# A fused recurrence, gated layer and soft mixture of experts: outputs in column parts for all token tiles, and another order of the same steps

## The chip, the cores and the metric

The kernel runs on one core of a Trainium2 chip, from loading the inputs in HBM to the last output byte in HBM, as one program. The metric is the device time of one execution in microseconds (us); smaller is better. The kernel before took 550.89 us, the median of three runs that lie between 550.50 and 551.18 us.

## The reference: what is computed

The inputs r, k, v, w have the shape [4, 8, 768, 48] (batch, heads, positions, features of a head), u has [8, 48], all float32. The weights w_in [384, 2048] and w_out [2048, 384] arrive as float64; phi [384, 32], w1 [8, 384, 1024] and w2 [8, 1024, 384] are float32. There are three parts.

```python
for t in range(S):                                   # 1. recurrence over 768 positions
    cur = einsum('bhd,bhe->bhde', u * k[t], v[t])
    y[t] = einsum('bhd,bhde->bhe', r[t], state + cur)
    state = w[t][..., None] * state + einsum('bhd,bhe->bhde', k[t], v[t])
x = y.transpose(0, 2, 1, 3).reshape(3072, 384)       # 3072 tokens
h = x @ w_in                                         # 2. gated layer
x = (h * cos(h)) @ w_out
logits = x @ phi                                     # 3. soft mixture of experts, 32 slots
d = softmax of logits over the 3072 tokens           #    (a column each)
slot_input = d.T @ x                                 #    [32, 384], 4 slots for each of 8 experts
slot_out[e] = relu(slot_input[e] @ w1[e]) @ w2[e]
c = softmax of logits over the 32 slots              #    (a row each)
out = c @ slot_out                                   #    [3072, 384] float32, 4.72 MB
```

Because d is a softmax over all tokens, no row of the output can be computed before the last token has gone through parts 1 and 2.

## The kernel before

**One list sets the order.** Most of the program is a string HEAD of 1977 names such as `h.11.5.0`, each a small function with its arguments. A loop runs through them inside `manual_schedule`, and every instruction then stands on its engine in the order in which the list issued it: an engine that waits for one of its instructions lets all later ones wait. The DMA triggers on SyncE (SP) go by the same list. After the list comes the tail, written out in Python, where order is set in the same way.

**Recurrence.** The tokens are cut into 24 blocks of 128 (two chunks of 64 in each head). For block j the steps are: loads (`lw`, `lk`, `lr`, `lv`, `lz`), transposes on TensorE (`wT`, `kT`, `rT`, `kN`), scans of the decays on VectorE (`scan`, L156, and `sp`), scaled keys and receptances (`ks`, `L`), the product of the two inside a chunk (`A`, TensorE) and its triangular mask (`mask`, L222, VectorE), the bonus sum (`ru` on GpSimd, `bo`, L243, on VectorE, `bv`), the update of the state (`U`, L259, TensorE, 0.88 us, then `z`, `st`, `rz`), the output (`y`, `yb`), and its two halves in a rounded format (`xh`, `xl`).

**Weights.** The float64 weights are turned into float32 on the chip by integer operations on their bits. For each of eight blocks n of w_in (`.i.n`) and of w_out (`.o.n`) the list has a load `raw`, a pass `abs` on ScalarE (L353), then `mx` (L357), `d1`, `d2a` and `d2b` (L374) on VectorE. Blocks of w_out are afterwards transposed on TensorE (`oT.m`, L416, three 128x128 tiles each, two of them per block), copied by ScalarE (`oc`) and multiplied by phi (`om`), so that the logits need only the product of g with w_out times phi.

**Gated layer.** The tokens are also cut into 12 groups g of 256. For each group and each of eight blocks i of 256 features, `h.g.i.mm` multiplies x by a half (mm) of the block: nine products of 256 columns, L462 to L464. Then `turns` (L474, ScalarE), `rest` (L478, VectorE), `cos` (L482, ScalarE) and `mul` (L486, VectorE) make g = h cos h. `gT` (L494) transposes g and `l.g.i` (L507) adds its share to the logits.

**Logits and softmax over tokens.** When a group's logits are complete, `sum`, `lc` (L520, TensorE), `max`, `exp`, `xt`, `xr` and `xd` make its exponentials with a running maximum; in the last group ScalarE does it in one step (L551). `dT` (L579) transposes them, `dc` copies the exponentials to dt (L586, ScalarE), `ltok` copies the logits by token (L592, VectorE), and `E.g.half` (L603) adds g times these weights to a sum E over all tokens, 16 products of 256 columns for each half of the eight i-blocks; `es` takes it out of PSUM.

**Tail.** After the list the sum E goes through w_out (slot_input), then through the eight experts: `hidden(e)` (w1, L797) and `expert_out(i, e)` (w2, L838) for the column part i. The parts are `parts = (0:256, 256:384)`. A finished part is copied from PSUM to `so`; `slots_out` (L845) spreads it to 96 rows and `slots_round` writes it to `sr` in a rounded format (f32r), so that the output product over 96 rows (weights `cr` in three pieces, slots `sr`) runs in that format; `cf` holds the float32 weights of the first four token tiles, and with them a tile is multiplied straight from `so`, without `sr`.

**Outputs before.** There are 24 tiles of 128 tokens. `store(i, tag, tiles, n)` multiplies some tiles (L870 in float32, L873 in whole rows of 384 columns, L875 for a column part), copies them from PSUM by ScalarE and VectorE in turn (L877), and issues one DMA (L880). Tiles 0 to 11 get their first 256 columns after `slots_round(0)`, with the second column part of the experts between them; tiles 0 and 1 use the float32 path. After `slots_round(1)` tiles 12 to 23 are written in whole rows, two tiles in each DMA, with two neighbouring tokens on a partition, and last the 128 columns of tiles 0 to 11, four tiles in each DMA. That makes 16 output DMAs.

## Time and profile before

| What | Value |
|---|---|
| Median of three runs | 550.89 us (550.50 to 551.18) |
| The profiled execution's own time | 552.63 us |
| Its span in the trace | 550.8 us, 16214 instructions |
| TensorE (PE) busy | 507.3 us, 92% |
| TensorE weight loads (PEld) busy | 437.9 us, 80% |
| VectorE (DVE) busy | 433.2 us, 79% |
| ScalarE (ACT) busy | 315.8 us, 57% |
| GpSimd (POOL) busy | 124.8 us, 23% |
| Mean granted TensorE clock | 0.968 of full |
| DMA | 67.52 MB, of which 4.72 MB written |

The span is the time from the first to the last event of the trace of one execution; the execution itself took 1.83 us more. Busy shares are averages over the whole span. PEld runs beside PE and is not added to it. A row of a timeline shows when an instruction, or a group of like ones, began and how long it was at work, and in brackets how long its engine had been idle before it and which engine's instruction let it go. A chain of waits is read back from the last instruction: each step is what released the next. `32x256` is partitions by elements, `x16` the number of instructions.

### The profile page before, as it was taken

How to read it: one execution, taken by the hardware profiler on the slowest of the kernel's cores; microseconds unless marked ns; L12 is line 12 of the kernel's file. 1: busy time of each engine (PE TensorE's matmuls, PEld its weight loads, DVE VectorE, ACT ScalarE, POOL GpSimd, SP SyncE). 2: the span in 40 equal slices, each digit the busy share in tenths (PEclk: the TensorE clock that was granted, in tenths of full speed). 3: DMA queues.
4: the chain of work that ended last, by engine and by line, in shares of the span. 5: the costliest groups of instructions: out<-in, count | busy, mean ns of one | idle time of the engine just before them, and what ended most of it. 6: DMA issues, size and time to landing. Idle time of an engine off the chain costs nothing.

```text
span 550.8 us, 16214 instructions
## 1 busy us (share of the span) xinstructions
PE 507.3 (92%) x6832; PEld 437.9 (80%) x6832; DVE 433.2 (79%) x825; ACT 315.8 (57%) x663; POOL 124.8 (23%) x163
## 2 busy tenths in 40 slices
PE   2759879989999999999999999999999999997994
PEld 1537668879898898998988989999899899874564
DVE  4989998997888879987878898989788777563413
ACT  3246567746757465576555765656566856655422
POOL 4520120254044122321320410623124000001300
PEclk9977998999999999999999999999999999997996
DMA  8994756444432523411441243173131692477937
GB/s 195 252 247 102 177 121 182 122 75 74 73 60 44 87 50 65 74 27 28 71 72 30 52 81 56 22 126 48 20 57 30 231 377 82 175 266 275 401 116 262
DMA packets 144360, 67.52 MB, mean 123 GB/s; under 512 B 127520, under 2 KB 131616, under 8 KB 144288
## 3 DMA queue, kind: packets, MB, share of 16 engines
q1 hardware_dynamic: 144288, 66.49, 47.8%
q8 instruction: 54, 0.88, 0.7%
q14 instruction: 18, 0.15, 0.1%
HBM read 61.75 MB, written 4.72 MB: 121 GB/s over the span
## 4 chain that ended last, share of the span: by engine, by line
PE 64%; DVE 16%; ACT 8%; DMA 5%; SPq 4%; issue 2%; ACTq 0%; DVEq 0%
PE h L462 9%; PE h L464 9%; PE h L463 9%; PE gT L494 6%; PE E L603 4%; PE l L507 3%; PE y L288 3%; PE A L208 3%; PE U L259 2%; PE so L838 2%; DMA rawi<-in_moe_w_in_dram 2%; PE hps L797 2%; DVE g L478 2%; DVE L L222 2%; ACT g L482 2%
## 5 line engine op out<-in xcount | busy, mean ns | idle before, releaser
L462 PE MATMUL h<-x,wu 128*128 128x256 f32 x573 | 171.8, 300 | 1.3 <-DVE g L486 1.3
L464 PE MATMUL h<-x,wu 128*128 128x256 f32 x573 | 161.0, 281 | 0.0
L463 PE MATMUL h<-x,wu 128*128 128x256 f32 x573 | 161.0, 281 | 0.0
L462 PEld LDWEIGHTS h<-x,wu 128*128 128x128 f32 x573 | 108.9, 190 | 3.5 <-DVE g L486 1.7
L463 PEld LDWEIGHTS h<-x,wu 128*128 128x128 f32 x573 | 109.1, 190 | 0.2
L464 PEld LDWEIGHTS h<-x,wu 128*128 128x128 f32 x573 | 108.7, 190 | 0.0
L482 ACT ACTIVATE g<-g,half_pi 128x512 f32<-128x512 f32 (+1 forms) x97 | 69.4, 719 | 42.6 <-DVE g L478 41.6
L486 DVE TENSOR_TENSOR g<-g,h 128x512 f32<-128x512 f32 x96 | 64.9, 678 | 27.8 <-ACT g L482 27.2
L474 ACT ACTIVATE g<-h 128x512 int32<-128x512 f32 x96 | 57.0, 596 | 40.0 <-PE h L464 33.0
L478 DVE SCALAR_TENSOR_TENSOR g<-g,h 128x512 f32<-128x512 int32 x96 | 65.0, 678 | 17.0 <-ACT g L474 15.8
L251 POOL TENSOR_TENSOR bv<-vz,bo 64x384 f32<-64x384 f32 x48 | 43.8, 912 | 140.5 <-DVE bo L243 54.4
L499 ACT COPY gt<-gT 128x512 f32<-128x512 f32 x92 | 53.4, 584 | 31.2 <-PE gT L494 30.6
L494 PE MATMUL gT<-cs,g 128*128 128x128 f32 x384 | 58.6, 277 | 0.2
L494 PEld LDWEIGHTS gT<-cs,g 128*128 128x128 f32 x384 | 44.1, 141 | 6.0 <-issue 3.3
L169 POOL TENSOR_TENSOR ru<-rn,u_b 128x384 f32<-128x384 f32 x24 | 26.8, 1118 | 58.5 <-issue 19.5
L193 POOL MEMSET L<- 64x512 f32 x32 | 16.7, 521 | 95.9 <-PE y L288 81.5
L156 DVE TENSOR_TENSOR_SCAN qt<-wf,one_b 128x520 f32<-128x520 f32 x24 | 31.1, 1297 | 7.3 <-ACT wf L151 7.3
L222 DVE TENSOR_TENSOR L<-A,cs 64x512 f32<-64x512 f32 x48 | 33.1, 689 | 3.5 <-PE A L208 2.4
L274 ACT COPY rzs<-z 64x192 f32<-64x192 f32 x96 | 33.4, 348 | 3.6 <-DVE z L269 2.6
L187 DVE TENSOR_TENSOR L<-rT,pt 64x512 f32<-64x512 f32 x48 | 32.9, 686 | 1.6 <-PE rT L141 0.6
L164 DVE TENSOR_TENSOR_SCAN pt<-wf,ini_f 128x520 f32<-128x520 f32 x24 | 31.7, 1321 | 0.1
L288 PEld LDWEIGHTS y<-L,rzs 128*32 128x32 f32 x1536 | 25.0, 112 | 6.6 <-ACT rzs L274 2.3
(176 smaller groups left out, 845.4 us busy)
## 6 DMA issues: line engine op xcount, KB each, us to landing
...
```

The source lines that it names most:

```text
L222: nc.vector.tensor_tensor(out=L[h, a], in0=ps[h], in1=mask[h].unsqueeze(1).to_broadcast([64, NS, C]), op=ALU.mult)
L251: nc.gpsimd.tensor_tensor(out=bv[h], in0=vn_t[j][h, :, c, :], in1=bo[h].to_broadcast([64, H, D]), op=ALU.mult)
L288: nc.tensor.matmul(ps[m:m + 32, o, c * C:(c + 1) * C], lhsT=rz[:, c, p, a, 32 * b:32 * b + 32], rhs=L[:, a, 2 * p + c, :], start=m not in ...
L462: nc.tensor.matmul(hp, lhsT=wh, rhs=xh[:, c, :], start=(c == 0), stop=False)
L463: nc.tensor.matmul(hp, lhsT=wh, rhs=xl[:, c, :], start=False, stop=False)
L464: nc.tensor.matmul(hp, lhsT=wl, rhs=xh[:, c, :], start=False, stop=(c == KD - 1))
L474: nc.scalar.activation(gt.bitcast(I32), hp, AF.Copy, bias=0.25, scale=1.0 / TWO_PI)
L478: nc.vector.scalar_tensor_tensor(out=gt, in0=gt.bitcast(I32), scalar=-TWO_PI, in1=hp, op0=ALU.mult, op1=ALU.add)
L482: nc.scalar.activation(gt, gt, AF.Sin, bias=half_pi[:, 0:1])
L486: nc.vector.tensor_tensor(out=gt, in0=gt, in1=hp, op=ALU.mult)
L494: nc.tensor.transpose(ps[:, tt, mm, :], gt[:, mm, tt * 128:(tt + 1) * 128], ident)
L499: (nc.vector.tensor_copy if NBK * g + i >= ATT and i in (1, 2) else nc.scalar.copy)(t, pend.pop(("gT", g, i)))
```

## The change

Two things are changed. In the tail, `store` and `copy_so` are replaced by `outputs(i, n0, tile_)`, and the calls after it are written in another order. Now all 24 tiles get their first 256 columns in twelve steps of two tiles (n0 = 0 to 11), most of them between the experts of the second column part, and after `slots_round(1)` come six steps of four tiles with the last 128 columns. The steps n0 = 0 and 1 of the first part are issued one tile at a time. The float32 path is used for the first four tiles, in both column parts. Each step has one DMA of its own, except n0 = 1 of the first part, whose two tiles share one; together there are 19. `so` is copied by one engine for each part (ScalarE for the first, VectorE for the second), and `expert_out(1, 0)` stands before the first output tile.

Second, HEAD holds the same 1977 names in another order. Its rows tell little by themselves; the first two stand for the rest.

```diff
--- before.py
+++ after.py
@@ -815,8 +815,7 @@
             for e in range(5):
                 hidden(e)
             sr = tw_p.tile([128, 3072], F32R, tag="tw", name="sr")[0:96, 0:DM]
-            crt = tw_p.tile([128, NT], F32R, tag="tw", name="cr")[0:96]
-            cr = crt.rearrange("p (j b t) -> p j b t", j=4, b=NB)
+            cr = tw_p.tile([128, NT], F32R, tag="tw", name="cr")[0:96].rearrange("p (j b t) -> p j b t", j=4, b=NB)
             for j in range(2):
                 for b in range(2):
                     weights(cr, j, b)
@@ -852,178 +851,172 @@
 
             obs = {}
 
-            def store(i, tag, tiles, n):
-
-                cols = slice(0, DM) if i is None else parts[i]
-                w = cols.stop - cols.start
-                if tag not in obs:
-                    obs[tag] = wu_p.tile([128, 3072], F32, tag=tag, name=f"ob{tag}")
-                ob = obs[tag][:, n * w:(n + len(tiles)) * w].rearrange("p (t f) -> p t f", f=w)
-                nb = max(1, 512 // w)
-                for b0 in range(0, len(tiles), nb):
-                    k = min(nb, len(tiles) - b0)
-                    ps = pb(f"o{tag}{tiles[b0]}_{w}")[:, 0:k * w].rearrange("p (t f) -> p t f", f=w)
-                    for t in range(k):
-                        tt = tiles[b0 + t]
-                        if tt < 2 and i == 0:
-
-                            nc.tensor.matmul(ps[:, t], lhsT=cf[:, tt * 128:(tt + 1) * 128], rhs=so[:, cols], start=True, stop=True)
-                        elif i is None:
-                            o = tiles[0] * 128 + b0 + t
-                            nc.tensor.matmul(ps[:, t], lhsT=crt[:, o:o + 255:2], rhs=sr[:, cols], start=True, stop=True)
-                        else:
-                            nc.tensor.matmul(ps[:, t], lhsT=crt[:, tt * 128:(tt + 1) * 128], rhs=sr[:, cols], start=True, stop=True)
-                    pend["ob"] = 1 - pend.get("ob", 0)
-                    (nc.scalar.copy if pend["ob"] else nc.vector.tensor_copy)(ob[:, b0:b0 + k], ps)
-                t0 = tiles[0] * 128
-                dst = out[t0:t0 + len(tiles) * 128, cols]
-                nc.sync.dma_start(dst.rearrange("(p t) f -> p t f" if i is None else "(t p) f -> p t f", p=128), ob)
-
-            def copy_so(i):
-                c, h = parts[i], (parts[i].start + parts[i].stop) // 2
-                nc.scalar.copy(so[:, c.start:h], ops[i][:, 0:h - c.start])
-                nc.vector.tensor_copy(so[:, h:c.stop], ops[i][:, h - c.start:c.stop - c.start])
+            def outputs(i, n0, tile_=None):
+
+                cols = parts[i]
+                n = cols.stop - cols.start
+                nt = 512 // n
+                t0, t1 = (0, nt) if tile_ is None else (tile_, tile_ + 1)
+                ps = pb(f"o{i}_{n0}_{t0}").rearrange("p (t f) -> p t f", t=nt)[:, 0:t1 - t0]
+                if n0 % 6 == 0 and t0 == 0:
+                    obs[i] = wu_p.tile([128, 6, nt, n], F32, tag=f"wu{n0 // 6 if i == 0 else 2}", name=f"ob{i}_{n0}")
+                ob = obs[i][:, n0 % 6, t0:t1]
+                for t in range(t0, t1):
+                    tt = n0 * nt + t
+                    if tt < 4:
+
+                        nc.tensor.matmul(ps[:, t - t0], lhsT=cf[:, tt * 128:(tt + 1) * 128], rhs=so[:, cols], start=True, stop=True)
+                    else:
+                        nc.tensor.matmul(ps[:, t - t0], lhsT=cr[:, tt // NB, tt % NB, :], rhs=sr[:, cols], start=True, stop=True)
+                if tile_ is not None and n0:
+                    nc.vector.tensor_copy(ob, ps)
+                    if t1 < nt:
+                        return
+                    ob, t0 = obs[i][:, n0 % 6], 0
+                else:
+                    (nc.vector.tensor_copy if n0 % 2 else nc.scalar.copy)(ob, ps)
+                nc.sync.dma_start(out[(n0 * nt + t0) * 128:(n0 * nt + t1) * 128, cols].rearrange("(t p) f -> p t f", p=128), ob)
 
             expert_out(0, 0)
             hidden_t(1)
             for e in range(1, NE):
                 expert_out(0, e)
-            copy_so(0)
-            store(0, "wu0", [0], 0)
+            nc.scalar.copy(so[:, parts[0]], ops[0][:, 0:256])
+            expert_out(1, 0)
+            outputs(0, 0, 0)
             slots_out(0)
-            store(0, "wu0", [1], 1)
             slots_round(0)
-            for e in range(2):
+            outputs(0, 0, 1)
+            outputs(0, 1, 0)
+            outputs(0, 1, 1)
+            for n0 in range(2, 5):
+                outputs(0, n0)
+            for e in range(1, 4):
                 expert_out(1, e)
-            for t in range(2, 8, 2):
-                store(0, "wu0", [t, t + 1], t)
-            for e in range(2, 5):
+            for n0 in range(5, 9):
+                outputs(0, n0)
+            for e in range(4, NE):
                 expert_out(1, e)
-            for t in range(8, 12, 2):
-                store(0, "wu0", [t, t + 1], t)
-            for e in range(5, NE):
-                expert_out(1, e)
-            copy_so(1)
+            nc.vector.tensor_copy(so[:, parts[1]], ops[1][:, 0:128])
+            for n0 in range(9, 12):
+                outputs(0, n0)
             slots_out(1)
             slots_round(1)
-            for t in range(12, 18, 2):
-                store(None, "wu1", [t, t + 1], t - 12)
-            for t in range(18, 24, 2):
-                store(None, "wu2", [t, t + 1], t - 18)
-            for t in range(0, 12, 4):
-                store(1, "wu3", [t, t + 1, t + 2, t + 3], t)
+            for n0 in range(6):
+                outputs(1, n0)
 
 
 
 HEAD = """
-lw.0 wT.0 wf.0 scan.0 z.0.0 raw.i.2 abs.i.2 mx.i.2 d1.i.2 sr.0 d2a.i.2 d2b.i.2 lk.0 kT.0 sp.0 raw.i.0.0 abs.i.0.0 mx.i.0.0 lr.0
-rT.0 L.0 misc ru.0 ks.0 lw.1 whi.2 wT.1 wf.1 scan.1 wn.2.0 wc.2.0 d1.i.0.0 raw.i.0.1 abs.i.0.1 lr.1 rT.1 wn.2.1 lk.1 lv.0 wc.2.1
...
+lw.0 wT.0 z.0.0 wf.0 raw.i.2 abs.i.2 scan.0 sr.0 lr.0 lw.1 rT.0 mx.i.2 sp.0 lk.0 d1.i.2 d2a.i.2 wT.1 kT.0 ks.0 raw.i.0.1 lw.2 lv.0
+wf.1 lk.1 L.0 A.0 d2b.i.2 whi.2 wn.2.0 kN.0 ksn.0 scan.1 mask.0 lr.1 rT.1 sr.1 sp.1 L.1 raw.i.0.0 misc ru.0 kT.1 U.0 ks.1
...
```

What the other order moves is shown at three places. The first is VectorE around the last block of w_out that is decoded. `ao` is the block on its way, `rawo` its float64 bits, `wo_sb` the decoded weights, `L` with `A` the masked product of block 5, `bo` the bonus sum of block 4. Before, VectorE's queue holds there:

```order
L187 TENSOR_TENSOR L_1362<-rT_1309,pt_1302 64x512 x2
L357 TENSOR_SCALAR ao_1316<-ao_1316 128x768
L361 TENSOR_SCALAR ao_1316<-ao_1316 128x768
L243 TENSOR_REDUCE bo_1384<-ru_1245 128x8
L486 TENSOR_TENSOR g_6_1221<-g_6_1221,h_6_1196 128x512
L222 TENSOR_TENSOR L_1362<-A_1365,cs 64x512 x2
L366 SCALAR_TENSOR_TENSOR ao_1316<-rawo_1256,ao_1316 128x768
L374 SCALAR_TENSOR_TENSOR wo_sb<-rawo_1256,ao_1316 128x768
L156 SCALAR_TENSOR_TENSOR qt_1433<-wf,one_b 128x520
```

It now holds:

```order
L374 SCALAR_TENSOR_TENSOR wo_sb<-rawo_1193,ao_1202 128x768
L478 SCALAR_TENSOR_TENSOR g_7_1313<-g_7_1313,h_7_1267 128x512
L357 TENSOR_SCALAR ao_1365<-ao_1365 128x768
L361 TENSOR_SCALAR ao_1365<-ao_1365 128x768
L366 SCALAR_TENSOR_TENSOR ao_1365<-rawo_1363,ao_1365 128x768
L374 SCALAR_TENSOR_TENSOR wo_sb<-rawo_1363,ao_1365 128x768
L486 TENSOR_TENSOR g_7_1313<-g_7_1313,h_7_1267 128x512
L222 TENSOR_TENSOR L_1329<-A_1345,cs 64x512 x2
L269 TENSOR_TENSOR z_0_1441<-st_state,qt_1140 128x192
L243 TENSOR_REDUCE bo_1447<-ru_1188 128x8
```

The mask and the bonus sum, which stood ahead of the last row with `wo_sb`, now stand behind it, and the g of an i-block stands around the decode. On TensorE three steps that stood ahead of the transpose `oT.14` of this block, `U.5`, `gT.0.6` and `oT.13`, now stand behind it.

The second place is TensorE at the end of the list, in the last group of tokens (l with g_4 to g_7 are products for its logits, lc their transpose, gT the transposes of its g, dT the transpose of its exponentials, and E with dt_7319 and dt_7318 the sum for the group before it). Before:

```order
L603 MATMUL E_7322<-gt_7_7264,dt_7319 32x256
L507 MATMUL l_7152<-g_4_7307,p_sb 32x256 x2
L507 MATMUL l_7152<-g_5_7275,p_sb 32x256 x2
L507 MATMUL l_7152<-g_6_7157,p_sb 32x256 x2
L507 MATMUL l_7152<-g_7_7236,p_sb 32x256 x2
L494 MATMUL gT_5_7359<-cs,g_5_7275 128x128 x4
L520 MATMUL lc_7364<-lg_7353,cs 128x256
L494 MATMUL gT_4_7368<-cs,g_4_7307 128x128 x4
L579 MATMUL dT_7388<-cs,dl_112 128x128
L494 MATMUL gT_7_7392<-cs,g_7_7236 128x128 x4
L603 MATMUL E_0_7410<-gt_0_7164,dt_7397 32x256
```

Now:

```order
L507 MATMUL l_7187<-g_6_7160,p_sb 32x256 x2
L507 MATMUL l_7187<-g_7_7309,p_sb 32x256 x2
L494 MATMUL gT_6_7351<-cs,g_6_7160 128x128 x4
L520 MATMUL lc_7362<-lg_7360,cs 128x256
L494 MATMUL gT_7_7373<-cs,g_7_7309 128x128 x4
L603 MATMUL E_7336<-gt_4_7093,dt_7318 32x256
L603 MATMUL E_7336<-gt_5_7196,dt_7318 32x256
L603 MATMUL E_7336<-gt_6_7145,dt_7318 32x256
L603 MATMUL E_7336<-gt_7_7091,dt_7318 32x256
...
L579 MATMUL dT_7390<-cs,dl_112 128x128
L494 MATMUL gT_4_7395<-cs,g_4_7274 128x128 x4
```

Half of the E of group 10 has moved from ahead of the logits to between `lc` and `dT`. Its 16 products are shown up to the first four; the logits of i-blocks 6 and 7 now end the logits.

The third place is TensorE in the last stage (so_7684 and so_7685 are the two column parts of the experts' output, sp the spread slots, owu and o_ the output tiles). Before:

```order
L838 MATMUL so_7684<-we_7579,wo_sb 32x256 x8
L870 MATMUL owu_256_7758<-wo_sb 128x256
L845 MATMUL sp_7762<-wo_sb,cs 96x256
L870 MATMUL owu_256_7764<-wo_sb 128x256
L838 MATMUL so_7685<-we_7408,wo_sb 32x128 x8
L838 MATMUL so_7685<-we_7421,wo_sb 32x128 x8
L875 MATMUL owu_256_7786<-sr,cr 128x256 x2
...
L838 MATMUL so_7685<-we_7579,wo_sb 32x128 x8
L845 MATMUL sp_7861<-wo_sb,cs 96x128
L873 MATMUL owu_384_7866<-sr,cr 128x384
L875 MATMUL owu_128_7910<-sr,cr 128x128 x4
```

Now:

```order
L837 MATMUL so_7684<-we_7579,wo_sb 32x256 x8
L837 MATMUL so_7685<-we_7429,wo_sb 32x128 x8
L868 MATMUL o_0_0_7764<-wo_sb 128x256
L844 MATMUL sp_7769<-wo_sb,cs 96x256
L868 MATMUL o_0_1_7773<-wo_sb 128x256
L868 MATMUL o_1_0_7777<-wo_sb 128x256
L870 MATMUL o_2_0_7784<-sr,cr 128x256 x2
...
L837 MATMUL so_7685<-we_7579,wo_sb 32x128 x8
L870 MATMUL o_11_0_7887<-sr,cr 128x256 x2
L844 MATMUL sp_7892<-wo_sb,cs 96x128
L868 MATMUL o_0_0_7896<-wo_sb 128x128 x4
```

The row of whole rows, `128x384`, is gone; the tiles with 256 columns stand ahead of the second `sp`, and behind it come only tiles with 128 columns, of which the first four read `wo_sb` (float32) and not `sr`.

## Rows read from the trace of the kernel before

**Rows 1.** Busy by stage: us, PE PEld DVE ACT POOL (instructions), PEclk, DMA, GB/s.

```profile
0.00:118.20 118.20, 90.31 (x1032) 71.86 (x1033) 103.99 (x161) 63.82 (x122) 30.54 (x47) 0.93 0.74 171
118.20:482.00 363.80, 360.61 (x5052) 326.65 (x5050) 301.80 (x597) 224.93 (x476) 87.53 (x107) 1.00 0.36 80
```

**Rows 2.** Waits of VectorE, 0 to 125 us: us in total, times, longest us.

```profile
DVE qt L156 <- ACT wf L151: 6.4, 1, 6.4
DVE ao L357 <- ACT ao L353: 3.3, 3, 1.6
DVE ai L357 <- ACT ai L353: 2.1, 3, 1.1
```

**Rows 3.** Timeline, last weight block: start us, us, what, [idle before <- releaser].

```profile
112.29 0.55 DVE L243 TENSOR_REDUCE bo<-ru 128x8 f32<-128x384 f32 x1
113.59 1.39 DVE L222 TENSOR_TENSOR L<-A,cs 64x512 f32<-64x512 f32 x2
115.88 1.67 DVE L374 SCALAR_TENSOR_TENSOR wo_sb<-rawo,ao 128x768 int32<-128x768 int32 x1
117.69 0.85 PE L416 MATMUL woT<-cs,wo_sb 128*128 128x128 f32 x6 [0.80 <-DVE wo_sb L374]
```

**Rows 4.** Timeline of block 0 (price of one U step).

```profile
22.68 0.88 PE L259 MATMUL U<-vz,ksn 128*64 128x96 f32 x16
```

**Rows 5.** Timeline at the end of the list, last group of tokens.

```profile
491.93 1.93 PE L603 MATMUL E<-gt,dt 128*32 128x256 f32 x32 [0.82 <-ACT dt L586]
499.35 0.48 PE L579 MATMUL dT<-cs,dl 128*128 128x128 f32 x1 [2.48 <-ACT dl L551]
499.87 0.47 DVE L592 COPY ltok<-dT 64x64 f32<-64x64 f32 x2 [2.82 <-PE dT L579]
500.42 0.42 ACT L586 COPY dt<-dT 64x64 f32<-64x64 f32 x2 [0.94 <-DVE ltok L592]
500.89 3.64 PE L603 MATMUL E<-gt,dt 128*32 128x256 f32 x32 [0.21 <-ACT dt L586]
```

**Rows 6.** Timeline of the half-width g steps of the last group.

```profile
486.55 0.36 ACT L474 ACTIVATE g<-h_7b 128x256 int32<-128x256 f32 x1
486.95 0.42 DVE L478 SCALAR_TENSOR_TENSOR g<-g,h_7b 128x256 f32<-128x256 int32 x1 [0.85 <-ACT g L474]
487.40 0.51 ACT L482 ACTIVATE g<-g,half_pi 128x256 f32<-128x256 f32 x1
487.94 0.42 DVE L486 TENSOR_TENSOR g<-g,h_7b 128x256 f32<-128x256 f32 x1 [0.57 <-ACT g L482]
```

**Rows 7.** Chain of waits, 469 to 475 us: start us, us, what.

```profile
469.36 1.73 PE E L603 x32
474.17 0.43 PE lc L520 x2
474.60 0.44 PE gT L494 x4
```

**Rows 8.** Timeline of the last stage.

```profile
530.80 16.22 SPq L880 DMA_DIRECT2D out_dram<-obwu  x16
531.16 1.08 PE L838 MATMUL so<-we,wo_sb 128*32 128x128 f32 x32
532.29 0.94 PE L875 MATMUL owu<-sr,cr 96*128 96x256 f32 x6
544.18 0.69 DVE L877 COPY obwu<-owu 128x512 f32<-128x512 f32 x1 [1.02 <-PE owu L875]
```

**Rows 9.** Busy time by stretch at the end; columns as in Rows 1.

```profile
534.00:536.00 2.00, 2.00 (x60) 1.67 (x52) 0.69 (x1) 0.59 (x1) 0.00 (x0) 1.00 0.86 282
544.00:546.00 2.00, 0.14 (x1) 0.00 (x0) 0.69 (x1) 0.00 (x0) 0.00 (x0) 0.50 1.03 389
546.00:548.00 2.00, 0.00 (x0) 0.00 (x0) 0.00 (x0) 0.00 (x0) 0.00 (x0) 0.50 0.99 309
548.00:551.00 3.00, 0.00 (x0) 0.00 (x0) 0.00 (x0) 0.00 (x0) 0.00 (x0) 0.50 0.49 132
```

More of the change, by code (lines that the diff above doesn't have):

```diff
@@ new lines @@
+cos.0.7 mul.0.7 h.1.0.1 mask.5 oT.14 oc.14 oT.15 oc.15 h.1.1.0 lz.5 z.5.0 oT.13 bo.4 gc.0.4 scan.6 kT.6 ks.6 l.0.5 bv.4 ru.6
+rz.4.1 oc.13 om.3 U.5 st.5.0 z.5.1 sr.6 st.5.1 turns.1.0 pc.3 pT.3 rz.5.0 gT.0.6 gc.0.6 rest.1.0 cos.1.0 ps.3 h.1.1.1 wT.7 sp.6
+y.4 mul.1.0 wf.7 scan.7 bo.6 rz.5.1 l.0.7 turns.1.1 sum.0 y.5 rest.1.1 cos.1.1 lc.0 yb.4 xh.4 ru.5 rT.6 h.1.2.0 h.1.2.1 sr.7
+mul.1.1 bo.5 max.0 turns.1.2 rest.1.2 h.1.3.0 h.1.3.1 z.6.0 L.6 exp.0 cos.1.2 mul.1.2 bv.5 yb.5 gT.0.7 A.6 gc.0.7 turns.1.3
@@ new lines @@
+E.1.1 y.8 lz.9 rz.9.0 cos.2.7 mul.2.7 l.2.7 gT.2.5 gc.2.5 h.3.1.0 h.3.1.1 turns.3.1 sum.2 gT.2.6 yb.8 h.3.0.0 gc.2.6 xh.8 es.1
+lr.11 lc.2 ru.10 bo.10 mask.9 gT.2.4 sp.10 wT.11 h.3.0.1 rest.3.1 cos.3.1 lv.10 lk.11 ru.11 bo.11 max.2 exp.2 z.9.1 st.9.1 wf.11
+mul.3.1 xl.8 xt.2 xr.2 kN.10 gc.2.4 rz.9.1 rT.10 zl.10 L.10 xd.2 ksn.10 turns.3.0 rest.3.0 h.3.2.0 h.3.2.1 dT.2 dc.2 ltok.2
+cos.3.0 z.10.0 gT.3.1 gc.3.1 cmb.0.0 turns.3.2 U.10 st.10.0 mul.3.0 rest.3.2 z.10.1 A.10 y.9 l.3.1 yb.9 xh.9 h.3.3.0 h.3.3.1
@@ new lines @@
+h.3.6.1 ru.12 bv.10 bo.12 turns.3.6 lv.12 lv.11 lk.14 gT.3.4 h.4.0.0 h.4.0.1 rest.3.6 cmb.0.2 cos.3.6 mul.3.6 rz.10.1 y.10 gc.3.4
+turns.4.0 ks.12 rest.4.0 l.3.7 sum.3 cos.4.0 gT.3.7 rT.12 mul.4.0 bv.11 zl.12 gc.3.7 lr.13 lw.14 L.12 z.12.0 h.4.1.0 h.4.1.1
+mask.11 turns.4.1 gT.3.6 gc.3.6 h.4.2.0 lw.13 wT.13 rest.4.1 cos.4.1 mul.4.1 U.11 st.11.0 lc.3 h.4.2.1 gT.3.2 wf.13 z.11.1 max.3
+turns.4.2 rest.4.2 st.11.1 h.4.3.0 gc.3.2 cos.4.2 yb.10 xh.10 gT.4.0 gc.4.0 mul.4.2 kN.12 scan.13 sr.13 exp.3 xt.3 h.4.3.1
@@ new lines @@
+bv.17 ru.16 lz.16 turns.6.2 lk.18 L.16 rest.6.2 A.16 U.16 xh.15 xl.15 z.16.0 cos.6.2 mul.6.2 turns.6.3 gc.6.0 gT.6.1 bo.16 zl.17
+rest.6.3 cos.6.3 mul.6.3 h.6.4.0 mask.16 h.6.4.1 gc.6.1 exp.5 xt.5 xr.5 xd.5 gT.6.3 turns.6.4 gc.6.3 rest.6.4 sr.17 cos.6.4
+h.6.5.0 rT.17 lr.19 lw.19 gT.6.2 h.6.5.1 lr.18 ru.18 st.16.0 z.16.1 rz.16.1 mul.6.4 st.16.1 rz.16.0 turns.6.5 dT.5 wT.18 lw.20
+kT.17 dc.5 sp.17 ltok.5 lz.17 L.17 rest.6.5 gc.6.2 ks.17 h.6.6.0 h.6.6.1 wf.18 scan.18 E.5.0 l.6.3 E.5.1 y.16 lz.18 cos.6.5
@@ L1027 @@
+l.11.3 turns.11.4 xd.10 dT.10 gT.11.3 gc.11.3 rest.11.4 h.11.7.0 cos.11.4 h.11.7.1 turns.11.7.0 turns.11.7.1 mul.11.5 gT.11.5
+dc.10 ltok.10 we.6 we.7 mul.11.4 l.11.5 rest.11.7.0 rest.11.7.1 cos.11.7.0 mul.11.7.0 E.10.0 cos.11.7.1 mul.11.7.1 l.11.7 gT.11.6
+gc.11.5 gc.11.6 sum.11 lc.11 max.11 quart.11 gT.11.7 E.10.1 exp.11 dT.11 dc.11 gT.11.4 ltok.11 E.11.0 gc.11.4 gc.11.7 es.10
+esl.11.0 E.11.1 esl.11.1 we.8 we.9
 """
```

193 lines of the change are left out of this document (87 added, 106 removed).

## The prediction

> **What bounds the kernel now.** I read the busy times by stage first, then VectorE's waits, then the timelines of the places where a stage ends. The reader is to see three regimes. Up to 118.2 us VectorE is the bound: it is busy 103.99 of 118.2 us and TensorE only 90.31 [rows 1]; VectorE's larger waits there are 6.4 us for the very first block and 3.3 and 2.1 us behind ScalarE's first pass over freshly loaded weights [rows 2]. From 118.2 to 482 us TensorE is the bound: 360.61 of 363.8 us busy [rows 1], so no order of the list can win more than 3.2 us there. After that the work thins out: TensorE waits 0.82 us and 2.48 us at the end of the list and then runs at half clock [rows 5], and in the last stage the chain ends in the copies and the output transfers: the last copy starts at 544.18 [rows 8], while the transfers stay full to 548 and take about half of the last stretch [rows 9].
>
> So the change has to be judged at four places: the start up to the last decoded weight block, the long middle, the end of the list, and the outputs.
>
> **Start.** VectorE's last decode step (w_out block 7) runs at 115.88 for 1.67 us, and TensorE waits 0.80 us for it [rows 3]. Both lists put the same VectorE steps ahead of that step, except two: the mask of block 5 (1.39 us) and one bonus sum of block 4 (0.55 us) [rows 3] now come behind it. The decode is thus 1.94 us earlier. But TensorE's transpose of that block (oT.14) also has three steps fewer ahead of it, and they must be done later: U.5 (0.88) [rows 4], gT.0.6 (0.44) [rows 7] and oT.13 (half of the 0.85 that two such transposes take, 0.43) [rows 3], together 1.75. What TensorE really gains is the difference: -0.2 us. The other waits of VectorE I leave as they are. The new list asks for the first w_out block with 0.9 us less VectorE work ahead of it, counted with the same durations, and with one load more in front of it, which makes a wait; it has ScalarE's third pass over w_out stand so that the buffer it needs is free, which takes one away. Bounds: all of the 3.3 and 2.1 us of such waits go (-5.4) or they double (+5.4) [rows 2]; I take 0.
>
> **Middle.** The same instructions, TensorE full. Bounds: the 3.2 us that are idle now [rows 1] go, or as much comes on top. Between a wide step h and the transpose or logits that use it, both lists leave TensorE work of about the length of the ScalarE and VectorE chain or more; I take 0.
>
> **End of the list.** Four things change.
> - The second half of E.10 (half of 1.73, 0.87 us) [rows 7] now stands behind the last logits. Before, both halves ran ahead of them [rows 5], and TensorE then sat idle 2.48 us before dT.11. The gap falls to 1.6 us: -0.87.
> - Behind dT.11 the slice copies to dt on ScalarE waited for the two ltok copies on VectorE: 0.47 us at 499.87, dt from 500.42, E.11 from 500.89 [rows 5]. dt now comes first, and E.11 follows dT.11 by the transpose between them: 0.5 us earlier.
> - E.10 waited 0.82 us for its dt [rows 5]. It now has the last two wide steps and more between dT.10 and itself: -0.82.
> - The last wide step is now h.11.7, in two halves, and its logits l.11.7 are close behind. Its chain takes 1.81 us from the first ScalarE step at 486.55 to the end of the product at 488.36 [rows 6], plus dt.10's 0.42 us on ScalarE, which stands between. Beside it lie gT (0.44), l.11.5 (0.43, as one f32 product of 256 columns) and half of E.10 (0.87) [rows 7]: 2.23 - 1.74 = 0.5 us of new waiting. The logits l.11.3 before it have a like chain behind two other ScalarE steps; between nothing and the 0.82 us of such a wait here I take 0.5.
>
> Sum: -0.87 - 0.5 - 0.82 + 1.0 = -1.2 us. Bounds: E.11 takes 3.64 us at half clock, where E took 1.73 at full clock [rows 5, 7]; if the shorter gap keeps the clock up, another -1.9. If every new wait is as long as the 2.48 us one, the gain is lost and 1.3 us more. I take the clock to fall as before, since 1.6 us of the idle time stay.
>
> **Outputs.** Before, 3.15 MB of the 4.72 MB (2.36 MB in whole rows, 0.79 MB in 128 columns) can only be computed after the second slot product is finished and rounded; transfers run at 0.86 of full in 534 to 536 and are full in 544 to 548 [rows 9]. Now 3.15 MB go out as 256 columns of all tiles, three quarters of them before that product is finished, and only the 128-column part (1.57 MB) depends on it. TensorE's own work does not set the end: after the first issue (530.80 before, taken as the same now) come one slot product and three f32 tiles (4 x 0.43) [rows 7] and six f32r tiles (0.94) [rows 8], and from about 533.2 the transfers are never out of work, with 0.26 MB sent. Rates: pieces of 1 KB 282 GB/s at 0.86, so 328; pieces of 512 B 309 at 0.99, so 312; whole rows 389 at 1.03, so 378 [rows 9]. 2.88 MB at 328 is 8.8 us, 1.57 MB at 312 is 5.0: the last byte at 547.0. Before it is at 549.5 (0.49 of the last 3 us) [rows 9]. That is -2.5 us.
>
> What hides the finer work: the 128-column products of seven experts (7 x 0.54 us) [rows 8], 14 f32r tiles at 0.16, one slot product, four half-width f32 tiles and 20 half-width tiles at no more than 0.16 bring the last copy to about 545.0, and the transfers want it by 546.2. Two more tiles in f32 cost TensorE half a microsecond, inside that 1.2 us. Without that cover each microsecond counts. Bounds: the 1 KB pieces go as fast as whole rows (8.8 becomes 7.6: -3.7), or all pieces only reach the 269 of the last stretch (132 GB/s at 0.49) [rows 9], which takes 16.5 us instead of 13.8: +0.2. I take -2.5, from the stretches whose pieces are the nearest in size.
>
> **Sum.** -0.2 + 0 - 1.2 - 2.5 = -3.9 us, on the span of 550.8 us: 546.9. The profiled execution took 552.63, 1.83 more than its span, and lies 1.74 above the median of the runs, 550.89; the difference is applied to that median: 547.0 us.
>
> **Rivals.**
> 1. Fine pieces cost nothing. If pieces of 512 B and 1 KB moved at the whole rows' 378 GB/s, 4.45 MB would take 11.8 us instead of 13.8, and the time would be 545.0. For it: 0.86 of full at 534 may be a queue that was short of work. Against it: two full stretches side by side show 389 and 309 GB/s [rows 9]. The Trainium skill says this in "DMA: Bandwidth & Descriptors", Specifications: transfers reach line rate from 512 B on. By that rule the time is this rival's 545.0; the trace does not agree, with 309 against 389 GB/s, and the measurement decides. A shorter gap that keeps the clock up ends at the same place (547.0 - 1.9 = 545.1). Together 0.08.
> 2. The output transfers eat the gain. 19 issues instead of 16, no piece larger than 1 KB, at 269 GB/s: +0.2 in place of -2.5, and 549.7. For it: the transfers, not TensorE, end the program [rows 8, 9]. Against it: 1.57 MB instead of 3.15 MB are left at the late point. 0.17.
> 3. The start gets slower. VectorE has no slack before the last decode, so each wait of it there goes through to the end. If the new order of loads doubles the 5.4 us that it waits behind ScalarE's first passes [rows 2], the sum is -3.9 + 5.4 = +1.5: 552.4. It decides from the point where the last decode step ends more than 3.9 us after 117.55. For it: less work ahead of the first w_out block and one more load. Against it: the same loads, and more work ahead of some w_in blocks. 0.22.
> 4. The forecast, 547.0, by itself 545.2 to 549.3: 0.53.
>
> **Numbers.** No change is within 0.2% (1.1 us), what a measurement of this kernel can tell. Rival 2 ends at the lower edge of that and is split. Faster: the forecast, rival 1 and 0.05 of rival 2, 0.66; within: the other 0.12 of rival 2; slower: rival 3, 0.22. The range takes in rivals 1 and 3 up to their named times: 544.6 to 552.4.
>
> **What would show it.** Right: the last w_out decode ends about 1.9 us earlier and TensorE's busy time up to its transposes is about 1.75 us less; between the last logits and dT.11 an E runs and the idle time before dT.11 is about 1.6 us; dt follows dT.11 without ltok between; output transfers full from about 533 after a first issue at the same distance from the slot product, and the last byte some 18 us after that product instead of 20.5. Wrong: VectorE's waits for loads above 7 us before the last decode; idle time of more than 3.2 us in the middle; transfers that run dry after 535; a last copy later than 546.

## The result, and the profile after

The changed kernel took 558.33 us (median of four runs, 557.09 to 560.10) where the kernel before took 551.00 (550.50 to 551.18) beside it: a ratio of 1.0137, 95% interval 1.0116 to 1.0159. It is slower by 7.3 us; the forecast was 547.0, in a range of 544.6 to 552.4. The profiled execution has a span of 558.3 us against 550.8.

To see where the time went I follow one quantity through both traces: by how much TensorE is **late**. It is the time at which a step begins on TensorE, less the time that all steps ahead of it in that kernel's own list take there at full clock (h 1.08 us a half, A 1.05, y 1.10, U 0.88, E 0.87 a half, l 0.50, transposes 0.33 to 0.46, from full stretches of the trace of before). While TensorE works without a pause this number stays still; it grows by each wait and by what half clock costs. From 172 to 280 us it stays between 44.1 and 44.5 in the kernel before, which shows that the prices fit. Every number of this kind comes from one execution. (At 82 us the kernel before stands just ahead of a wait of 2.43 us for a load of v; behind it the two kernels are about 2 us apart, not 4.4.)

| Late, us | 20 us | 55 us | 82 us | 131 us | 172 us | 280 us | 390 us | 485 us |
|---|---|---|---|---|---|---|---|---|
| before | 16.1 | 31.9 | 37.0 | 44.5 | 44.2 | 44.5 | 46.3 | 47.5 |
| after | 15.1 | 32.7 | 41.4 | 48.1 | 50.2 | 51.7 | 53.6 | 57.5 |

So the start cost 3.6 us (44.5 to 48.1), and the middle, from 131 to 485 us, 6.4 (it grew by 9.4 in place of 3.0). The end of the list up to the first step of the tail gave back 1.1 (5.9 after 485 us in place of 7.0), and from the first w2 product to the end of the span it took 28.0 in place of 29.5 us: 1.5 gained. Together 3.6 + 6.4 - 1.1 - 1.5 = 7.4 of the 7.5 us.

The busy times by stretch, after (columns as in [rows 1]):

```profile
0.00:118.20 118.20, 90.62 (x1002) 72.11 (x1003) 102.72 (x157) 62.18 (x119) 25.14 (x43) 0.91 0.72 168
118.20:482.00 363.80, 354.48 (x4994) 318.24 (x4992) 301.10 (x587) 216.49 (x463) 97.55 (x110) 1.00 0.37 79
```

Beside [rows 1] the middle shows it at once: TensorE is idle for 9.3 us of this stretch where it was idle for 3.2. VectorE's work there is the same. The start looks alike in busy time, but with a clock of 0.91 in place of 0.93 and fewer instructions done (1002 for 1032).

The waits of VectorE from 0 to 125 us, after, and its decode of w_in block 6 and of the last w_out block (start us, us, what):

```profile
DVE ai L357 <- ACT ai L353: 2.5, 2, 1.8
DVE x L313 <- ACT x L309: 1.8, 2, 1.2
DVE g L486 <- ACT g L482: 1.3, 1, 1.3
DVE ao L357 <- ACT ao L353: 1.0, 2, 0.6
```

```profile
79.63 1.46 DVE L374 SCALAR_TENSOR_TENSOR ai<-rawi,ai 128x768 int32<-128x768 int32 x1
117.90 0.96 DVE L374 SCALAR_TENSOR_TENSOR wo_sb<-rawo,ao 128x768 int32<-128x768 int32 x1
```

The waits of [rows 2] behind ScalarE's first passes did not double, they fell from 5.4 to 3.5 us. The last decode ended at 118.86, 1.3 us later than in [rows 3], not 1.9 earlier. The blocks ahead of it were later still: w_in block 6 ended at 81.1 us, where before it ended at 74.3 (VectorE, before):

```profile
73.32 0.95 DVE L374 SCALAR_TENSOR_TENSOR ai<-rawi,ai 128x768 int32<-128x768 int32 x1
```

The end of the list, after (timeline of TensorE):

```profile
502.80 0.64 PE L507 MATMUL l<-g,p_sb 128*32 128x256 f32 x8 [1.55 <-DVE g L486]
506.73 1.07 PE L603 MATMUL E<-gt,dt 128*32 128x256 f32 x16
509.51 0.33 PE L579 MATMUL dT<-cs,dl 128*128 128x128 f32 x1 [1.71 <-ACT dl L551]
510.35 3.12 PE L603 MATMUL E<-gt,dt 128*32 128x256 f32 x32
```

Against [rows 5], half of E.10 fills the gap, which is 1.71 us (forecast 1.6, before 2.48); E.11 begins 0.84 us behind dT.11 in place of 1.54; the new wait of the logits is 1.55 us.

The output transfers, after; the last two stretches have pieces of 512 B (columns as in [rows 1]):

```profile
542.00:544.00 2.00, 2.00 (x54) 1.80 (x47) 0.57 (x2) 0.47 (x2) 0.00 (x0) 1.00 0.77 253
544.00:546.00 2.00, 2.00 (x64) 1.87 (x66) 1.04 (x2) 1.06 (x2) 0.00 (x0) 1.00 1.06 344
546.00:548.00 2.00, 2.00 (x27) 1.80 (x20) 1.50 (x3) 0.75 (x2) 0.00 (x0) 1.00 1.00 328
552.00:554.00 2.00, 0.00 (x0) 0.00 (x0) 0.00 (x0) 0.00 (x0) 0.00 (x0) 0.50 1.04 287
554.00:556.00 2.00, 0.00 (x0) 0.00 (x0) 0.00 (x0) 0.00 (x0) 0.00 (x0) 0.50 1.06 289
```

Whole pieces of 1 KB go at 328 to 344 GB/s, as forecast (328); pieces of 512 B at 287 to 289, not 312. And in 542 to 544 us, from 2.2 us behind the first issue (539.82), the transfers are only 0.77 busy.

### The profile page after: what moved, and what is told of

Read it like the earlier page. It is cut to its first block, busy times and chain, and to the rows that moved or that the text cites. A ratio compares the mean times of both kernels' runs of the same rounds, so it can differ in the third digit from the quotient of the medians.

```text
span 558.3 us, 16224 instructions
## 1 busy us (share of the span) xinstructions
PE 510.1 (91%) x6850; PEld 438.8 (79%) x6850; DVE 437.7 (78%) x823; ACT 312.6 (56%) x660; POOL 129.4 (23%) x163
## 4 chain that ended last, share of the span: by engine, by line
PE 57%; DVE 25%; ACT 7%; DMA 4%; issue 3%; SPq 3%; POOL 0%; ACTq 0%; DVEq 0%; POOLq 0%
PE h L462 8%; PE h L463 8%; PE h L464 8%; PE gT L494 5%; PE l L507 3%; PE E L603 3%; DVE g L478 3%; PE y L288 3%; DVE g L486 3%; DVE L L222 2%; PE A L208 2%; DVE L L187 2%; PE hps L797 2%; PE so L837 2%; PE U L259 2%
## 5 line engine op out<-in xcount | busy, mean ns | idle before, releaser
L486 DVE TENSOR_TENSOR g<-g,h 128x512 f32<-128x512 f32 x96 | 65.1, 679 | 26.5 <-ACT g L482 26.0
L251 POOL TENSOR_TENSOR bv<-vz,bo 64x384 f32<-64x384 f32 x48 | 44.4, 925 | 114.9 <-PE kT L141 41.5
L507 PE MATMUL l<-g,p_sb 128*32 128x256 f32 x384 | 30.1, 385 | 2.6 <-DVE g L486 2.6
L170 POOL TENSOR_TENSOR ru<-ru,kn 128x384 f32<-128x384 f32 x24 | 29.8, 1243 | 9.0 <-DMA kn<-in_k_dram 7.3
L208 PEld LDWEIGHTS A<-L,ks 128*64 128x64 f32 (+1 forms) x768 | 26.3, 144 | 6.1 <-issue 3.7
```

What stands on the lines that cost most here:

```text
L251: nc.gpsimd.tensor_tensor(out=bv[h], in0=vn_t[j][h, :, c, :], in1=bo[h].to_broadcast([64, H, D]), op=ALU.mult)
L486: nc.vector.tensor_tensor(out=gt, in0=gt, in1=hp, op=ALU.mult)
L507: nc.tensor.matmul(lps_t[g][32 * mm:32 * mm + 32, 0:G], lhsT=p_sb[:, m, :], rhs=g_t[g, m // 2][:, m % 2, :], start=(m < 4), stop=(m >= MF ...
```

## The experiments

Sixteen kernels were run, four at a time on one chip beside runs of the kernel before. "Late" is read from each one's profiled execution; "growth" is from 131 to 485 us, "end" from there to the first step of the tail, "outputs" from the first w2 product to the end of the span.

| Run | Ratio to before (95%) | Late at 131 | Growth | End | Outputs |
|---|---|---|---|---|---|
| before | | 44.5 | 3.0 | 7.0 | 29.5 |
| after | 1.0137 (1.0116 to 1.0159) | 48.1 | 9.4 | 5.9 | 28.0 |
| a | 0.9965 (0.9943 to 0.9987) | 42.8 | 2.8 | 5.3 | 27.9 |
| b | 1.0157 (1.0122 to 1.0193) | 45.3 | 9.5 | 4.9 | 29.7 |
| c | 1.0088 (1.0056 to 1.0120) | 47.7 | 3.8 | 6.6 | 27.9 |
| d | 1.0081 (1.0056 to 1.0106) | 44.7 | 8.2 | 5.0 | 27.9 |
| e | 1.0078 (1.0050 to 1.0105) | 45.0 | 6.7 | 5.0 | 27.8 |
| f | 0.9967 (0.9948 to 0.9987) | 41.5 | 1.2 | 7.6 | 27.8 |
| g | 1.0095 (1.0060 to 1.0130) | 46.9 | 2.9 | 6.6 | 27.8 |
| h | 0.9985 (0.9968 to 1.0002) | 43.6 | 2.5 | 6.3 | 28.6 |
| i | 1.0090 (1.0058 to 1.0122) | 44.6 | 8.3 | 5.0 | 28.5 |
| j | 0.9924 (0.9902 to 0.9947) | 44.6 | 1.4 | 6.4 | 27.7 |
| k | 0.9936 (0.9914 to 0.9958) | 41.8 | 1.9 | 6.3 | 27.9 |
| l | 0.9942 (0.9920 to 0.9963) | 44.0 | 2.5 | 5.2 | 27.7 |
| m | 1.0138 (1.0106 to 1.0169) | 49.0 | 10.7 | 6.2 | 28.0 |
| n | 0.9988 (0.9971 to 1.0004) | 42.2 | 4.7 | 6.3 | 27.7 |
| s | 1.0091 (1.0065 to 1.0117) | 46.2 | 9.9 | 4.9 | 28.4 |
| u | 1.0099 (1.0070 to 1.0129) | 44.0 | 9.1 | 6.4 | 28.6 |

The same order does not start alike in every execution: the start of before (before, a, d, f, j, k, l, n) is 41.5 to 44.7 us late at 131 us, that of after (after, b, c, e, g, m) 45.0 to 49.0. Growth repeats better: 2.5 to 3.8 in the six with before's middle unchanged (before, a, c, g, h, l), 8.2 to 9.9 in the five with after's (after, b, d, i, s). Part of the spread is that the stretch is fixed in time: between the same two steps (those of before at 131 and 485 us) the six take 353.8 to 354.2 us.

**Which part (a to d).** Outputs and list apart, and the list cut at om.3, the last step on decoded weights.

```diff
a:  HEAD of before, tail of after
b:  HEAD of after, tail of before
c:  HEAD of after up to om.3, then what is left in before's order; tail of after
d:  HEAD of before up to om.3, then what is left in after's order; tail of after
```

> The list of before with the outputs of after, nothing else. Reading of the two traces: with the work that stands ahead of a step in its list subtracted, TensorE is late by 44.8 us (before) and 48.2 us (after) at 131 us, by 47.4 and 57.5 at the last group but one, and then wins back 1.2 us at the end of the list and 1.5 us from the first output on. Theory 1 (the losses are the list's, the outputs alone win): 551.0 - 1.5 = 549.5 us. Theory 2 (19 finer transfers and the new tail cost time by themselves, and the list is not to blame for all): 551 us or more.

> The list of after with the outputs of before. Theory 1 (the parts add up: start +3.4, middle +6.8, end of list -1.2): 551.0 + 9.0 = 560.0 us. Theory 2 (the outputs of after are part of the loss): below 558.3 us.

> The list of after up to the last step on decoded weights (om.3), the steps that are left in the order of before; outputs of after. Theory 1 (what the start loses stays lost, and the middle loses by its own order): 551.0 + 3.4 - 1.5 = 552.9 us. Rival 3 (the late start is what makes TensorE wait in the middle, the middle's order is innocent): 551.0 + 10.2 - 1.5 = 559.7 us. Rival 4 (the middle absorbs what the start loses): 549.5 us.

> The list of before up to the last step on decoded weights (om.3), the steps that are left in the order of after; outputs of after. Theory 1 (start and middle each lose by their own order): 558.3 - 3.4 = 554.9 us, with TensorE's waits in the middle as in after (about 9 us). Rival 3 (the middle waits because the start was late): 548.3 us. Rival 4: 558.3 us.

The outputs gain by themselves (a: 0.9965; 27.7 to 28.6 us in all kernels with them, 29.5 and 29.7 in the two without), and the list loses by itself (b). The middle loses by its own order: d, with the old start, grows by 8.2, and c, late by 47.7 at 131 us, only by 3.8. Rival 3 of run c is thereby excluded, though c's time, 555.8 us where before takes 551.0, lies between theory 1 (552.9) and that rival (559.7). The times of a, b and d came within 0.6 us of theory 1. c and d lie 6.8 and 6.4 us above a, 13.2 together, the whole list only 9.5. The difference of 3.7 us is more than the four intervals of 1.2 to 1.8 us make together if they are independent (2.8 us), so the two losses do not simply add: in time the new start costs 6.8 us ahead of the old middle (c less a) and 3.1 ahead of the new one (after less d), each within some 2 us.

**The middle (e, m, n).** Three places stand out in the trace of after. The first, on SyncE (a DMA issue that lasts as long as it is held up), GpSimd, VectorE and TensorE:

```profile
140.22 15.90 SPq L123 DMA_DIRECT2D vz<-in_v_dram  x4
160.27 1.02 POOL L169 TENSOR_TENSOR ru<-rn,u_b 128x384 f32<-128x384 f32 x1 [4.78 <-DMA rn<-in_r_dram]
163.39 0.55 DVE L243 TENSOR_REDUCE bo<-ru 128x8 f32<-128x384 f32 x1 [3.75 <-POOL ru L170]
165.82 0.66 PE L494 MATMUL gT<-cs,g 128*128 128x128 f32 x4 [1.32 <-ACT gt L499]
```

In the new list bv.6 stands behind bv.7 on GpSimd. lv.8 must wait until bv.6 has read the buffer, lr.8 waits behind lv.8 in SyncE's queue, ru.8 for lr.8, and VectorE stands 3.75 us at bo.8, with the g step that TensorE needs queued behind it. The third place is ScalarE's table of functions (the second, z.11.0 and L.11 between rest and mul of g step 3.5 at 220 to 224 us, is of the kind of the other gaps):

```profile
394.72 1.28 ACT L699 ACT_TABLE_LOAD   x1
397.72 1.28 ACT L556 ACT_TABLE_LOAD   x1
402.96 0.62 PE L507 MATMUL l<-g,p_sb 128*32 128x256 f32 x4 [1.03 <-DVE g L486]
```

The step `tab` loads the table of the exponential in the middle of steps that need the other one, which is loaded again 3 us later; nothing uses it before the next change, and the load ahead of the last exponential (L551) is in the trace of every kernel, with tab and without it.

```diff
e:  HEAD of after
-   tab
    bv.6   from behind bv.7 to ahead of ru.7
    L.11   from ahead of mul.3.5 to behind it
m:  e, and in the middle each mul.g.i as soon behind its cos as 0.7 us
    of VectorE's steps lie between rest and mul (24 moved)
n:  HEAD of before without tab, ltok.4 behind ks.15, same rule (20 moved)
```

> The kernel after with three edits in its list, each at one place where TensorE waits in the middle: the step that loads the table of the exponential function (tab) is left out (it writes a scratch number that nothing reads); bv.6 stands ahead of ru.7 on GpSimd, so that the load lv.8 does not hold SyncE's queue; L.11 stands behind mul.3.5 on VectorE. Theory 1 (each wait has its own cause in the order round it): what TensorE is late by grows by 0.3 us or less in place of 2.0 (160 to 172 us), 1.7 (215 to 230 us) and 2.9 (400 to 412 us); sum -6.2 us against the kernel after, so 552.1 us where before takes 551.0. Theory 2 (VectorE has no room in the middle, a wait that is taken away comes back at the next place): the middle still loses about 9 us in all, 557 us or more.

> The new list with the three moves in its middle (run e), and there, by one rule, 24 products mul of the g steps moved ahead of VectorE's other steps: mul stands as soon behind its cos as 0.7 us of VectorE's steps lie between rest and mul (27 us of steps are passed in all). Theory 1 (the order of VectorE between rest and mul makes TensorE wait in the middle): what TensorE is late by grows by 4 us or less from 131 to 485 us, in place of 6.7 in run e; about 3 us less than run e. Theory 2 (VectorE as a whole has too little room in this order: a step put first makes a scan or a mask late): it grows by 6 us or more.

> The old list without tab and with ltok.4 behind ks.15, outputs of after, and the same rule for mul in its middle (20 moved, 26 us of steps passed). Theory 1: the growth of 131 to 485 us falls from 1.2 to 1.9 us to 1 us or less, 546.5 us or a little under it. Theory 2: it grows by more than 2 us, 548 us or more.

Run e gave back 2.7 us of growth, not 6.2. Without tab the growth from 400 to 412 us was 0.6 in place of 3.0 and stayed away. TensorE's order is the same in these lists, so the time between the same two steps can be compared directly: after's 400 to 412 us take 11.6 to 12.1 us in the five kernels with tab there (after, b, d, i, s) and 9.2 to 9.7 in the three without (e, m, u). The two moves gave less: from 145 to 172 us e takes 0.9 us less than after, and from 215 to 280 us, round L.11, 65.1 us where after takes 65.0, so that this gain came back whole. Runs m and n suggest why. In run m (VectorE, then TensorE):

```profile
154.47 0.69 DVE L486 TENSOR_TENSOR g<-g,h 128x512 f32<-128x512 f32 x1 [2.02 <-ACT g L482]
155.54 1.38 DVE L187 TENSOR_TENSOR L<-rT,pt 64x512 f32<-64x512 f32 x2
157.07 1.63 PE L208 MATMUL A<-L,ks 64*64 64x64 f32 x32 [2.64 <-DVE L L187]
```

The product put first waits 2.02 us for its cosine, L stands behind it, and TensorE waits 2.64 us for L. With the rule the growth rose in both lists, to 10.7 (from 6.7) and 4.7 (f and j have 1.2 and 1.4 with the same two edits). Theory 2 of these runs holds: VectorE, busy 301 of 364 us in after, waits and does its steps in one queue, and what is put first makes another step late.

**The start (g, h, i, s, u).** Cutting at the decode of w_in block 3 (d2b.i.3, about 65 us), then taking away waits.

```diff
g:  HEAD of after up to d2b.i.3, then what is left in before's order; tail of after
h:  HEAD of before up to d2b.i.3, after's order up to om.3, then before's; tail of after
i:  after, with  abs.o.3 behind ksn.1,  mx.o.3 behind U.1,  oc.3 ahead of abs.i.4
s:  i, with  d2b.i.0.1 behind d2b.i.0.0,  ks.2 ahead of d2a.o.0
u:  m and s together
```

> The list of after up to the decode of w_in block 3 (about 68 us), the rest in the order of before; outputs of after. At 131 us TensorE is late by about 44 us under the old order and 47 under the new one. Theory 1 (the start loses behind this point, where GpSimd's steps for blocks 2 and 3 run beside the decode of w_in blocks 6, 5 and 7 and VectorE's steps beside them take 2 to 3 us longer): 44 us late, 549.4 us as with the list of before. Theory 2 (it loses ahead of this point, in the order of the first blocks): 47 us late, 552.4 us.

> The list of before up to the decode of w_in block 3 (about 65 us), the order of after from there to the last step on decoded weights (om.3), the rest in the order of before; outputs of after. Theory 1 (the start loses in this stretch): TensorE 47 us late at 131 us, 552.4 us, and VectorE's steps between 65 and 85 us take 2 to 3 us more than alone. Theory 2 (it loses ahead of it): 44 us late, 549.4 us.

> The kernel after with two places of its start changed on ScalarE: abs.o.3, which waits there for its 1.5 MB of w_out, stands behind ksn.1 (with mx.o.3 on VectorE behind U.1), and oc.3 ahead of abs.i.4, which waits for its weights. In the five runs with the new start TensorE stands still there 1.7 to 4.4 us ahead of wT.2 (26 to 28 us) and 0.6 to 2.8 us ahead of om.0 (56 to 58 us), and is 46.6 us late at 131 us in the mean (45.0 to 48.1); in the five with the old start 43.4 (41.5 to 44.7). Theory 1 (what the start loses is these two waits of TensorE behind ScalarE's waits for weights): both fall under 0.8 us, 43.5 us late at 131 us, 3 us less than the kernel after. Theory 2 (the later decode on VectorE decides, and waits of TensorE that are taken away come back): the two waits fall, but it stays at 45.5 us late or more at 131 us.

> Run i (ScalarE's order at two places of the new start) with two more moves on VectorE: d2b.i.0.1 right behind d2b.i.0.0 and ks.2 ahead of d2a.o.0. In run i TensorE stood still 6.9 us until the decoded w_in block 0 at 34.7 us and 2.7 us until ks.2 at 46.4 us. Theory 1 (these four waits are what the new start loses): 43.4 us late at 131 us as in the mean of the old start. Theory 2 (the waits only move, the decode as a whole runs later): 44.6 us late or more, as in run i.

> Runs m and s together: the new list with all moves of its start and its middle. Theory 1: 43.4 us late at 131 us, 4 us or less of growth to 485 us, the end and the outputs of after (-1.4 and -1.7 us against before): 548 us where before takes 551. Theory 2: 44.6 and 6: 552 us or more.

The loss arises ahead of 65 us: g is 46.9 us late at 131 us (ratio 1.0095), h 43.6 (0.9985). In time g lies 6.1 us above h, within some 2 us, and 3.8 above theory 2; one trace of each shows only 3.3 of it at 131 us. My theory of GpSimd's steps beside the decode of w_in blocks 6, 5 and 7 falls: h has after's order there and loses nothing that can be told. What stands there in after is ScalarE waiting for weights, with copies that TensorE needs behind it (ScalarE, then TensorE):

```profile
55.98 0.89 ACT L353 ACTIVATE ai<-rawi 128x768 f32<-128x768 f32 x1 [2.86 <-DMA rawi<-in_moe_w_in_dram]
57.29 1.49 PE L429 MATMUL pt<-wt,phi_sb 128*32 128x128 f32 x18 [2.46 <-ACT wt L422]
```

In run i this wait and the one ahead of wT.2 were gone or down to 0.73 us, but another grew to 6.87 us (2.8 to 4.4 in the six runs without these moves). It ends at 34.74 us, where it ended at 34.29 in after: TensorE came earlier and waited for the same decoded block.

```profile
25.08 0.65 PE L141 MATMUL wT<-cs,wn 128*128 128x128 f32 x4 [0.73 <-ACT ksn L238]
34.74 2.05 PE L404 MATMUL wl<-ai,cs 128*128 128x512 f32 x2 [6.87 <-DVE ai L374]
```

Lateness at 131 us was 44.6, 46.2 and 44.0 in i, s and u, 44.9 in the mean, against 47.0 in the mean of the six runs without these moves and 43.3 in that of the eight with before's start. So the moves may have given some 2 of 3.7 us. The ranges overlap, but the times point the same way: i and s lie 2.6 and 2.5 us below after, each within about 2 us, though after did not run beside them; u lies 2.1 us below m, which has the same middle and ran beside it, within 2.4. Run s with two more moves was no better than i. Run u missed theory 1 in its middle (growth 9.1 in place of 4) and in time (556.5 us where before takes 551); its 44.0 us at 131 us lie between the two theories, and one execution can't tell them apart.

**What holds on the old list (f, j, k, l).**

```diff
    all: HEAD of before, tail of after
k:  - tab
l:  E.10.1 between gT.11.4 and dT.11;  dc.10 behind dT.10;  dc.11 behind dT.11
j:  k and l, and ltok.4 behind ks.15
f:  - tab, ltok.4 behind ks.15, from dT.10 on what is left in after's order
```

> The list of before up to dT.10 with the end of the list and the outputs of after, tab left out, and ltok.4 behind ks.15 on VectorE (TensorE waited 1.3 us for ks.15 at 286.7 us in the kernel before, where ltok.4 waited 2.1 us ahead of it). Theory 1 (gains of separate places add): 551.0 - 1.65 (outputs) - 1.2 (end of list) - 1.0 (table loads at 431 to 437 us) - 1.5 (ltok.4) = 545.6 us. Theory 2 (gains in the middle come back as later waits): 548.1 us, the outputs and the end alone.

> The list of before with the outputs of after, without tab, with ltok.4 behind ks.15, and at the end E.10.1 between gT.11.4 and dT.11, dc.10 right behind dT.10 and dc.11 right behind dT.11. Theory 1 (each gain holds): -1.65 (outputs) - 0.8 (tab) - 0.6 (ltok.4) - 0.7 (end: dt no longer behind ltok; the move of E.10.1 gives nothing, since the logits then wait for the last g) = 547.3 us where before takes 551.0. Theory 2 (only the outputs' gain holds): 549.4.

> The list of before without tab, with the outputs of after. Theory 1 (three table loads of 1.28 us each at 431 to 437 us on ScalarE cost TensorE about 0.8 us): what TensorE is late by grows by 0.3 in place of 1.0 us from 437 to 455 us, 548.6 us. Theory 2 (ScalarE has room for them): 549.4 us.

> The list of before with only the three moves at its end (E.10.1, dc.10, dc.11 as in the run with four moves), outputs of after. Theory 1: TensorE's wait ahead of dT.11 falls from 2.5 to 1.6 us, a wait of about the same length appears ahead of the logits l.11.5 or l.11.7, and E.11 follows dT.11 after 0.8 in place of 1.4 us: 549.4 - 0.7 = 548.7 us. Theory 2 (the move of E.10.1 gives its whole 0.87 us as well): 547.8 us.

In the kernel before the step tab costs three table loads on ScalarE:

```profile
430.79 1.28 ACT L699 ACT_TABLE_LOAD   x1
433.28 1.28 ACT L482 ACT_TABLE_LOAD   x1
436.40 1.28 ACT L630 ACT_TABLE_LOAD   x1
```

Without it TensorE's growth from 437 to 455 us falls from 1.0 (a) to 0.3 (k), as theory 1 had it, and the ratio is 0.9936 against 0.9965 for a, with intervals that overlap. The Trainium skill states in "ScalarE activation tables: per-element evaluation and per-set limits", What a function is on this engine, that two functions in different sets are one load of 1283 ns apart; the trace agrees, 1.28 us each. Run l has the waits that theory 1 forecast: 1.48 us ahead of dT.11 in place of 2.48, a new wait of 1.03 ahead of its logits, and E.11 0.84 us behind dT.11. Its end takes 5.2 us against 5.3 in a, in both of which E.11 took 2.15 us; the 6.3 to 6.6 of c, g, h and k hold an E.11 of 3.0 to 3.5 us. So the traces show 0.1 us of the 0.7 forecast. The time, 547.8 us where before takes 551 (ratio 0.9942), would fit theory 2, which the new wait speaks against; its interval overlaps that of a. The move of ltok.4 gave 0.6 us between the same steps at 280 to 300 us (j against a), as j expected; f expected 1.5. Run j, with all of it, is the fastest kernel of the study: 545.63 us where before took 550.35, ratio 0.9924. Its lead over k and l is within the intervals. Run f shows that a part of one order does not fit into another: with after's end behind before's dT.10 the end took 7.6 us, 2.3 more than in a, which is more than the 1.6 of growth that tab and ltok.4 had gained.

## Why the prediction was wrong, step by step

- **Middle, "I take 0", bounds of 3.2 us either way: the step that failed most in the traces.** That TensorE is full for 360.61 of 363.8 us says what another order can win, and I took the same number for what it can lose. The trace held no such bound: TensorE was full because VectorE's queue happened to deliver each g in time. The reason given for 0, that TensorE has work of the length of the g step's chain between h and the step that uses its g, counts the chain alone and not the other steps that stand in VectorE's queue, such as bo.8 with its wait of 3.75 us. Measured: +6.4 us in the two traces; growth of 8.2 to 9.9 against 2.5 to 3.8. In time the new rest of the list costs 6.4 us behind the old start (d less a) and 2.7 behind the new one (after less c), each within some 2 us, so the times do not tell whether the middle or the start lost more.
- **Start, -0.2.** I compared the two lists at one point, the last decoded block, where VectorE's work ahead is 1.9 us less. For the blocks before it the new list has more VectorE work ahead (1.1 to 2.4 us for w_in block 7 and w_out blocks 4 to 6, by the same durations), and they came about 6 us later. Measured +3.6 us between the two traces, 3.1 to 6.8 in the times of the runs. Rival 3 named the place and, with 552.4, the sign, but not the mechanism: VectorE's waits behind ScalarE's first passes fell; TensorE was the one that waited, and which order ahead of 65 us does it is not settled.
- **End of the list, -1.2.** Right in sum (-1.1), partly by luck. The gap is 1.71 for 1.6 forecast, E.10's wait is gone, dt comes 0.70 us earlier for 0.5, and the new wait of the last logits was 1.55 us where I had 1.0 for two: together -0.7. Another -0.5 is E.11, 3.12 us in place of 3.64, whose clock I had taken to fall as before; it took 2.15 in b, d, e, f, i and s behind the same gap and 3.55 in m and u.
- **Outputs, -2.5.** Right in sign, mis-sized: -1.5 between the traces, -1.6 in the mean of the runs. Pieces of 512 B moved at 288 GB/s for 312, 0.4 us on 1.57 MB, and transfers were 0.77 busy in the stretch in which I had them full, 0.5 us. The 312 was misread: 546 to 548 us of before still held the last whole rows, 0.23 MB in pieces of 3 KB (two rows each, the 74 packets that are not under 2 KB). DMA packets of before from 546 to 548 us:

```profile
DMA packets 867, 0.62 MB, mean 309 GB/s; under 512 B 32, under 2 KB 793, under 8 KB 867
```

Only the last stretch of before, 548 to 551 us, was pure, and its 269, which I used as a bound, is near the 273 to 276 that 287 and 289 GB/s at 1.04 and 1.06 give here. Rival 1 (fine pieces cost nothing) is excluded by 288 against 328 to 344 in full stretches side by side, rival 2 (+0.2) by run a. The range's lower edge, 544.6, is not the time that rival 1 names, 545.0.

What stays open: tab explains 1.7 of the 6.4 us that the middle loses (it cost 2.4 in after, run e, and 0.7 in the list of before, run k), the chain from bv.6 about 1, and a pause of TensorE inside a product h another (last section). The rest, about 3 us, is spread over some six places where VectorE's order seems to let a g step or a scan come late, and the one rule tried made it worse, so which feature of the order decides was not found.
